# 48 of the 128 pieces of wo's last row on three partitions, loaded ahead of the rest of wo by three DMA engines

## The chip, the cores and the metric

The kernel runs on one core of one Trainium2 chip. The metric is the device time of one execution in microseconds; lower is better. The kernel before takes 382.13 us (median of three runs, 381.94 to 382.17). Its profiled execution took 382.16 us, and the profile's span of it is 380.7 us long.

The engines are called PE (TensorE, matrix products), DVE (VectorE), ACT (ScalarE), POOL (GpSimd) and SP (SyncE, which here only issues DMA transfers). SBUF is the memory on the chip in which all tiles lie, with 128 partitions; PSUM receives the results of PE. One core has sixteen DMA engines, which share the work of every large transfer.

## The reference, cut to what matters

One token `x` of 1024 features goes through two branches, which a gate mixes. Branch A is attention of 32 query heads over a cache of 65,536 keys and values in four groups of heads; branch B is a gated MLP for one position. All inputs are bf16.

```python
def reference(A_x, A_k_cache, A_v_cache, A_wq, A_wo, B_x, B_w_in, B_w_sp, B_b_sp, B_w_out, gate_w):
    # A_k_cache, A_v_cache: [1, 4, 65536, 128]; A_wq: [1024, 4096]; A_wo: [4096, 1024]
    def _A_ref(x, k_cache, v_cache, wq, wo):
        q = (x @ wq) as 32 heads of 128                     # (shortened)
        k, v = k_cache, v_cache repeated 8 times over heads  # (shortened)
        scores = jnp.einsum('bhqd,bhkd->bhqk', q, k) * Dh ** (-0.5)
        p = _softmax(scores, axis=-1)
        o = jnp.einsum('bhqk,bhkd->bhqd', p, v)
        return o.reshape(B, Sq, Hq * Dh) @ wo                # (transposes left out)
    ...
    g = _sigmoid((x * gate_w).sum(-1, keepdims=True))
    a = _A_ref(x, A_k_cache, A_v_cache, A_wq, A_wo)
    b = _B_ref(x, B_w_in, B_w_sp, B_b_sp, B_w_out)
    return g * a + (1 - g) * b
```

The last step of branch A, a vector of 4096 times `wo`, is what the change touches.

## The kernel before

All large inputs pass through one SBUF tile, `kv`, of five slots of 16,384 bf16 elements per partition. SP issues every load in program order into it; a load waits until the slot's former contents have been read. The order is: w_in, wq, the first K tiles, w_out, then K and V by groups, the last group's V in three loads, and last `wo` in five.

```python
P = 128
CT = 128
NKV = 5
...
WO_SPLIT = (24, 4, 2, 1, 1)
WO_BUSY = {24: 0, 4: 2, 2: 1, 1: 0}
...
    kv = big.tile([P, NKV * CT * P], BF16, name="kv")

    def load(src, shape, at):
        ...
        v = kv[:, int(at * CT * P):int(at * CT * P) + n]
        ...
        ins = nc.sync.dma_start(out=v, in_=src)
        ...
        return v
```

`wo` is seen as 128 partitions of 32 rows (partition p holds rows 32p to 32p+31 of `wo`), so a "row of wo" below is one row index c of all 128 partitions: 128 pieces of 1024 bf16 elements, 2 KB each, 256 KB in all. `project` multiplies one such row after the other with the attention output `oa` [128, 32], in four column blocks which go to four 32-row strips of PSUM, and adds it all up in `out_ps`. `keep_busy` issues matmuls on old data whose result nobody reads.

```python
    def keep_busy(n):
        ps = pss.tile([P, 2 * HN], FP32, name="busy_ps", tag="s")
        w = wt[G % 2][:].rearrange("p v b t u h -> p (v b t u h)")
        for i in range(n):
            ins = nc.tensor.matmul(ps[:, :HN], lhsT=w[:, :P], rhs=w[:, :HN], start=True,
                                   stop=True, skip_group_check=True)
            if i > 0:
                same_weights(ins)          # the repeated weight load is dropped

    NO = D // NB                           # 256
    out_ps = psl.tile([P, NO], FP32, name="out_ps")

    def project(w, n, vec, c0, first=False, last=False):
        for c in range(n):
            for t in range(NB):            # NB = 4
                nc.tensor.matmul(
                    out_ps[t * B:(t + 1) * B, :],
                    lhsT=vec[:, c0 + c:c0 + c + 1].to_broadcast([P, B]),
                    rhs=w[:, c, t * NO:(t + 1) * NO],
                    start=(first and c == 0), stop=(last and c == n - 1),
                    skip_group_check=True)
```

The end of the kernel: the last group's V in slots 2 and 3, then slot 1, then slot 0; the attention output; `wo` in rows of 24, 4, 2, 1 and 1 from slot 3 on; and the store.

```python
    for j, n, at in ((0, 2, 2), (2, 1, 1), (3, 1, 0)):
        for i, vt in enumerate(load_kv(A_v_cache, G - 1, j, at, n)):
            v_tile(G - 1, j + i, vt)
    keep_busy(6)
    head_out(G - 1)
    keep_busy(16)


    wo_view = A_wo.rearrange("(p c) n -> p c n", c=OC)      # OC = 32
    c0 = 0
    for n in WO_SPLIT:
        t = load(wo_view[:, c0:c0 + n, :], (n, D), 3 + c0 * D / (CT * P))
        project(t, n, oa, c0, last=(c0 + n == OC))
        keep_busy(WO_BUSY[n])
        c0 += n
    out_sb = const.tile([P, NO], BF16, name="out_sb")
    ...
    nc.scalar.copy(out=out_sb[:], in_=out_ps[:])
    for i, queue in enumerate((nc.scalar, nc.sync)):
        ...                                # two stores of 1 KB
```

`head_out(g)` (not shown) normalises the attention output of one group on DVE and PE, and writes `oa`. At the start the token and `gate_w` are loaded by ACT's queue as 8 partitions of 256 bytes each, and two single numbers (`B_w_sp`, `B_b_sp`) as one element each.

Of the kernel before, what the change touches and what calls it, by code (L numbers as in the profile page):

```python
# [8 lines left out]
FP32 = mybir.dt.float32  # L9
BF16 = mybir.dt.bfloat16  # L10
I32 = mybir.dt.int32
ACT = mybir.ActivationFunctionType
ALU = mybir.AluOpType
AX = mybir.AxisListType
# [4 lines that stand above are left out]
B = 32  # L19
NB = P // B  # L20
VC = 4
CC = CT // VC
ZN = 448
HN = 512
WO_SPLIT = (24, 4, 2, 1, 1)
WO_BUSY = {24: 0, 4: 2, 2: 1, 1: 0}


# [1 line left out]
def kernel(  # L30
# [15 lines left out]
    nc = tc.nc  # L46

    _, _, D = A_x.shape
    _, G, S, DH = A_k_cache.shape
# [7 lines left out]
    OC = HD // P  # L57
# [3 lines left out]
    NHB = HD // (NB * HN)  # L61
# [1 line left out]
    SCALE = float(DH) ** -0.5  # L63
    assert NB * VC * REP == P and G * B == P and B == REP * QD and DH == P and D % P == 0
    assert S % (P * CT) == 0 and F == 2 * NB * ZN and ZN == B * FC and HD == NHB * NB * HN
    assert NHB * NB == 2 * G and CC * B == 2 * HN and sum(WO_SPLIT) == OC

    const = ctx.enter_context(tc.tile_pool(name="const", bufs=1))
    wk = ctx.enter_context(tc.tile_pool(name="wk", bufs=2))
# [4 lines left out]
    psm = ctx.enter_context(tc.tile_pool(name="psm", bufs=1, space=bass.MemoryType.PSUM))  # L74
# [5 lines left out]
    def same_weights(ins):  # L80
        held.add(ins.ins.name)
# [93 lines left out]
    kv = big.tile([P, NKV * CT * P], BF16, name="kv")  # L175

    def load(src, shape, at):
        n = 1
        for s in shape:
            n *= s  # L180
        v = kv[:, int(at * CT * P):int(at * CT * P) + n]
        if len(shape) == 2:
            v = v.rearrange("p (a b) -> p a b", b=shape[1])
        ins = nc.sync.dma_start(out=v, in_=src)  # L184
        if not first_load:
            first_load.append(ins.ins.name)
        return v

    def load_kv(src, g, j, at, n=1):
        h, i = divmod(j, 2)  # L190
        rows = src[0, g, 2 * h * CT * P:2 * (h + 1) * CT * P, :].rearrange(
            "(p c) d -> p (c d)", c=2 * CT)
        v = load(rows[:, i * CT * DH:(i + n) * CT * DH], (n * CT * DH,), at)
        return [v[:, i * CT * DH:(i + 1) * CT * DH] for i in range(n)]
# [18 lines left out]
    row = const.tile([P, P], FP32, name="row")  # L213
    nc.gpsimd.iota(row[:], pattern=[[1, P]], base=0, channel_multiplier=0,
                   allow_small_or_imprecise_dtypes=True)
    pidx = const.tile([P, 1], I32, name="pidx")
# [7 lines left out]
    for t in wt:  # L224
        nc.gpsimd.memset(t[:], 0.0)

    pbits = const.tile([P, 6], I32, name="pbits")
    for i, m in enumerate((P // KC - 1, B - 1, QD - 1, REP - 1)):
        nc.vector.tensor_scalar(out=pbits[:, i:i + 1], in0=pidx[:], scalar1=m, scalar2=None,
                                op0=ALU.bitwise_and)  # L230
    nc.vector.tensor_scalar(out=pbits[:, 4:5], in0=pidx[:], scalar1=B.bit_length() - 1,
                            scalar2=None, op0=ALU.logical_shift_right)
    nc.vector.tensor_scalar(out=pbits[:, 5:6], in0=pidx[:], scalar1=REP.bit_length() - 1,
                            scalar2=2 * VC - 1, op0=ALU.logical_shift_right, op1=ALU.bitwise_and)
    pf = const.tile([P, 7], FP32, name="pf")
    nc.vector.tensor_copy(out=pf[:, 0:1], in_=pidx[:])
    nc.vector.tensor_copy(out=pf[:, 1:7], in_=pbits[:])

    def one_hot(shape, dtype, in0, col, name):
        t = const.tile(shape, dtype, name=name)  # L240
        nc.vector.tensor_scalar(out=t[:], in0=in0, scalar1=pf[:shape[0], col:col + 1],
                                scalar2=None, op0=ALU.is_equal)
        return t
# [9 lines left out]
                     start=True, stop=True)  # L253
    xm = const.tile([P, 2, KC, P // KC], FP32, name="xm")
    for t in range(2):
        nc.vector.tensor_tensor(  # L256
            out=xm[:, t], in0=xb_ps[:, t * P:(t + 1) * P].rearrange("p (i c) -> p c i", c=KC),
            in1=sel_i[:].unsqueeze(1).to_broadcast([P, KC, P // KC]), op=ALU.mult)
# [17 lines left out]
                            op0=ALU.add)  # L276
    nc.vector.reciprocal(out=gw[:, 2:3], in_=gw[:, 1:2])
    nc.vector.tensor_scalar(out=gw[:, 5:6], in0=gw[:, 2:3], scalar1=-1.0, scalar2=1.0,
                            op0=ALU.mult, op1=ALU.add)
# [4 lines left out]
    nc.vector.tensor_copy(out=own_bb[:], in_=own_b[:].unsqueeze(1).to_broadcast([P, NB, B]))  # L284
    own_8 = one_hot([P, 2 * VC], FP32, row[:, :2 * VC], 6, "own_8")
    own_q = one_hot([P, QD], FP32, row[:, :QD], 3, "own_q")
    hsel = one_hot([P, REP, QD], FP32, row[:, :REP].unsqueeze(2).to_broadcast([P, REP, QD]), 4,
                   "hsel")

# [20 lines left out]
    for hf in range(2):  # L310
        nc.vector.tensor_tensor(
            out=zm[:, hf], in0=z_ps[:, hf * HN:hf * HN + ZN].rearrange("p (j c) -> p j c", c=FC),
            in1=own_b[:].unsqueeze(2).to_broadcast([P, B, FC]), op=ALU.mult)
    z = wk.tile([P, 2 * FC], FP32, name="z")
    nc.vector.tensor_reduce(out=z[:].rearrange("p (h c) -> p h c", h=2),
                            in_=zm.rearrange("p h j c -> p h c j"), axis=AX.X, op=ALU.add)
# [3 lines left out]
                            op0=ALU.mult, op1=ALU.add)  # L320
# [4 lines left out]
                            op0=ALU.mult, op1=ALU.add)  # L325
# [12 lines left out]
                            scalar2=None, op0=ALU.mult)  # L338
    nc.vector.tensor_tensor(out=stat[:, 2:3], in0=stat[:, 0:1], in1=stat[:, 0:1], op=ALU.mult)
    nc.vector.tensor_tensor(out=stat[:, 3:4], in0=stat[:, 1:2], in1=stat[:, 2:3],  # L340
                            op=ALU.subtract)
    nc.vector.tensor_scalar(out=stat[:, 4:5], in0=stat[:, 3:4], scalar1=1e-5, scalar2=None,
                            op0=ALU.add)
# [4 lines left out]
                            op0=ALU.subtract, op1=ALU.mult)  # L348
    nc.vector.tensor_scalar(out=z2n[:], in0=z2n[:], scalar1=wsp, scalar2=bsp,
                            op0=ALU.mult, op1=ALU.add)  # L350
    uT = const.tile([P, FC], BF16, name="uT")
    nc.vector.scalar_tensor_tensor(out=uT[:], in0=zg[:, 0:FC], scalar=gate1, in1=z2n[:],
                                   op0=ALU.mult, op1=ALU.mult)
# [40 lines left out]
    oa = const.tile([P, OC], BF16, name="oa")  # L394
# [54 lines left out]
    def v_tile(g, j, vt):  # L449
        if j == 0:  # L450
            o_ps[g] = pso.tile([P, 2, VC * DH], FP32, name="o_ps")
        vx = vt.rearrange("p (v c d) -> p c v d", v=VC, d=DH)
        for u in range(CC // 2):
            hs = slice(u % 2 * P // 2, (u % 2 + 1) * P // 2)
            for e in range(2):
                ins = nc.tensor.matmul(  # L456
                    o_ps[g][hs, e, :],
                    lhsT=ptt[g, j][:, 2 * u:2 * u + 2, :].rearrange("p c x -> p (c x)"),
                    rhs=vx[:, 2 * u + e], start=(j == 0 and u < 2),
                    stop=(j == NT - 1 and u >= CC // 2 - 2), skip_group_check=True)  # L460
                if e > 0:
                    same_weights(ins)
# [35 lines left out]
                same_weights(ins)  # L498
# [4 lines left out]
    def project(w, n, vec, c0, first=False, last=False):  # L503
        for c in range(n):
            for t in range(NB):
                nc.tensor.matmul(  # L506
                    out_ps[t * B:(t + 1) * B, :],
                    lhsT=vec[:, c0 + c:c0 + c + 1].to_broadcast([P, B]),
                    rhs=w[:, c, t * NO:(t + 1) * NO],
                    start=(first and c == 0), stop=(last and c == n - 1),  # L510
                    skip_group_check=True)
# [3 lines left out]
    for j, n, at in ((0, 1, 2), (1, 1, 3), (2, 1, 0), (3, 1, 1)):  # L515
        for i, kn in enumerate(load_kv(A_k_cache, 0, j, at, n)):
            k_tile(0, j + i, kn)
        if j == 1:
            build_w(1)
    project(load(B_w_out.rearrange("(p c) n -> p c n", c=FC), (FC, D), 4), FC, uT, 0, first=True)  # L520
    stats(0)
    for g in range(1, G):
# [12 lines left out]
    for j, n, at in ((0, 2, 2), (2, 1, 1), (3, 1, 0)):  # L535
        for i, vt in enumerate(load_kv(A_v_cache, G - 1, j, at, n)):
            v_tile(G - 1, j + i, vt)
    keep_busy(6)
    head_out(G - 1)
    keep_busy(16)  # L540


    wo_view = A_wo.rearrange("(p c) n -> p c n", c=OC)
    c0 = 0
    for n in WO_SPLIT:
        t = load(wo_view[:, c0:c0 + n, :], (n, D), 3 + c0 * D / (CT * P))
        project(t, n, oa, c0, last=(c0 + n == OC))
        keep_busy(WO_BUSY[n])
        c0 += n
    out_sb = const.tile([P, NO], BF16, name="out_sb")  # L550
    out_rows = out.rearrange("o t (q n) -> (o t q) n", n=NO)
    nc.scalar.copy(out=out_sb[:], in_=out_ps[:])  # L552
# [5 lines left out]
    last = {}  # L558
# [37 lines left out]
```

## Time and profile before

| What | Value |
| --- | --- |
| time | 382.13 us (381.94 to 382.17) |
| span of the profile | 380.7 us, 2605 instructions |
| PE busy | 233.2 us (61%), 1395 matmuls |
| DVE busy | 218.5 us (57%) |
| ACT busy | 39.6 us (10%) |
| packets of the DMA engines | 3943, of 162.17 MB |
| chain that ended last, by engine | DMA 57%, PE 26%, DVE 13%, ACT 2% |

How to read it: busy time is an average over the whole span, so a share of 61% doesn't say that PE has slack at each point. The chain follows the last instruction back to what released it, step by step, and tells whose work set the end. A transfer is listed at its issue, and its length runs to its landing; much of that is time in the queue behind other transfers.

In the timeline a row has: start in us, length in us, engine, line, operation, tile written and tiles read, shape, count, and in brackets the idle time before it and what ended it.

### The profile page before, as it was taken

Reading aid. Unit: us, or ns where it says so; the run is one execution under the profiler, and the core shown is the slowest. Engines: PE = TensorE matmul, PEld = TensorE weight load, DVE = VectorE, ACT = ScalarE, POOL = GpSimd, SP = SyncE. Lnnn points to the kernel's source line nnn. Section 1 sums busy time; section 2 is a strip of 40 time slices with the busy share of each in tenths; the row PEclk is TensorE's granted clock in tenths of the full one; section 3 lists DMA queues with packets and bytes.
Section 4 is the critical chain, followed back from the end, with each engine's and each line's share of the span. In section 5 each row is a group of like instructions: output and inputs, shape, how many; then the busy total and the mean of one; then the engine's idle time right before and its main releaser. Section 6 shows DMA issues by size and latency. Waiting matters only on the chain.

```text
span 380.7 us, 2605 instructions
## 1 busy us (share of the span) xinstructions
PE 233.2 (61%) x1395; PEld 56.0 (15%) x800; DVE 218.5 (57%) x211; ACT 39.6 (10%) x55; POOL 4.4 (1%) x10
## 2 busy tenths in 40 slices
PE   0060657876157944796397729871977196839386
PEld 0010101111101210111011101120211011202113
DVE  4133288997597506966977059669970388460040
ACT  1001001110601100114010001050100000500000
POOL 4000000000000000000000000000000000000000
PEclk9995769899759895989688958895989579969789
DMA  9998999999999999999999999999999999999995
GB/s 386 496 420 379 411 438 441 437 483 430 387 420 441 441 436 441 427 441 441 434 436 441 441 427 434 406 423 441 434 434 429 420 441 442 436 410 430 424 443 223
DMA packets 3943, 162.17 MB, mean 426 GB/s; under 512 B 472, under 2 KB 476, under 8 KB 860
## 3 DMA queue, kind: packets, MB, share of 16 engines
q1 hardware_dynamic: 3892, 162.01, 98.8%
q8 instruction: 8, 0.13, 0.1%
q14 instruction: 3, 0.02, 0.0%
q10 hardware_dynamic: 40, 0.01, 0.0%
HBM read 162.01 MB, written 0.00 MB: 426 GB/s over the span
## 4 chain that ended last, share of the span: by engine, by line
DMA 57%; PE 26%; DVE 13%; ACT 2%; issue 1%; SPq 1%; DVEq 0%; ACTq 0%
DMA kv<-in_A_k_cache_dram 43%; PE s_ps L410 21%; DMA kv<-in_A_wo_dram 7%; DVE kv L403 7%; DMA kv<-in_A_v_cache_dram 7%; PE o_ps L456 4%; DVE pt L446 2%; DVE o_sb L470 1%; DVE mx L405 1%; ACT sc L421 1%; ACT sc L443 1%; DVE rowt L466 1%; SPq L184 1%; PE om_ps L476 0%; DVE osum L486 0%
## 5 line engine op out<-in xcount | busy, mean ns | idle before, releaser
L410 PE MATMUL s_ps<-kv,wt 128*128 128x512 bf16 x512 | 141.8, 437 | 80.2 <-DVE kv L403 80.2
L403 DVE STREAM_TRANSPOSE kv<-kv 128x2048 int32<-128x2048 int32 x64 | 142.7, 2281 | 54.3 <-DMA kv<-in_A_k_cache_dram 54.3
L456 PE MATMUL o_ps<-kv,pt 128*64 128x512 bf16 x512 | 61.7, 400 | 7.6 <-DMA kv<-in_A_v_cache_dram 7.6
L410 PEld LDWEIGHTS <-wt 128*128 128x128 bf16 x256 | 27.6, 108 | 195.6 <-issue 138.5
L421 ACT CAST sc<-s_ps 128x1024 bf16<-128x1024 f32 x16 | 16.2, 1012 | 249.9 <-PE s_ps L410 249.9
L456 PEld LDWEIGHTS <-pt 128*64 128x64 bf16 x256 | 16.1, 115 | 50.6 <-issue 48.1
L446 DVE STREAM_TRANSPOSE pt<-sc 128x1024 bf16<-128x1024 bf16 x16 | 18.6, 1217 | 6.8 <-ACT sc L443 6.8
L405 DVE TENSOR_REDUCE mx<-sc 128x1 f32<-128x1024 bf16 x12 | 14.5, 1210 | 9.9 <-ACT sc L421 9.9
L443 ACT ACTIVATE sc<-sc,nb 128x1024 bf16<-128x1024 bf16 x16 | 18.2, 1137 | 12.3 <-DVE nb L439 12.2
L466 DVE TENSOR_TENSOR rowt<-o_ps,own 128x1024 f32<-128x1024 f32 x4 | 4.8, 1195 | 24.9 <-PE o_ps L456 24.9
L476 PE MATMUL om_ps<-o_sb,hsel 128*32 128x128 f32 x8 | 2.3, 386 | 18.3 <-DVE o_sb L470 18.3
L425 DVE TENSOR_REDUCE mx<-sc 128x1 f32<-128x1024 bf16 x4 | 4.9, 1220 | 13.6 <-ACT sc L421 13.6
L296 PE MATMUL q_ps<-kv,xT 128*32 128x512 bf16 x64 | 5.6, 527 | 7.2 <-DMA kv<-in_A_wq_dram 7.2
L252 PE MATMUL xb_ps<-xg,spread 8*128 8x256 bf16 x1 | 0.4, 366 | 13.2 <-DMA xg<-in_gate_w_dram 13.2
L470 DVE TENSOR_REDUCE o_sb<-rowt 128x128 f32<-128x1024 f32 x4 | 7.5, 1872 | 0.1
L363 DVE TENSOR_TENSOR rowt<-q_ps,own_b 128x512 f32<-128x512 f32 x2 | 1.3, 686 | 10.8 <-PE q_ps L296 10.8
L296 PE MATMUL z_ps<-kv,xT 128*32 128x448 bf16 x64 | 5.9, 560 | 0.0
L495 PE MATMUL busy_ps<-wt 128*128 128x512 bf16 x23 | 5.8, 381 | 0.1
L506 PE MATMUL out_ps<-kv,oa 128*32 128x256 bf16 x128 | 4.2, 274 | 2.0 <-DMA kv<-in_A_wo_dram 2.0
L256 DVE TENSOR_TENSOR xm<-xb_ps,sel_i 128x128 f32<-128x128 f32 x2 | 0.5, 287 | 8.0 <-PE xb_ps L252 8.0
L552 ACT CAST out_sb<-out_ps 128x256 bf16<-128x256 f32 x1 | 0.4, 372 | 45.1 <-PE out_ps L506 45.1
L296 PEld LDWEIGHTS <-xT 128*32 128x32 bf16 x64 | 2.6, 136 | 14.6 <-issue 14.6
(90 smaller groups left out, 59.3 us busy)
## 6 DMA issues: line engine op xcount, KB each, us to landing
kv<-in_A_k_cache_dram SPq DMA_DIRECT2D x4, 4096.0 KB, 35.4
kv<-in_A_v_cache_dram SPq DMA_DIRECT2D x2, 4096.0 KB, 26.0
kv<-in_B_w_in_dram SPq DMA_DIRECT2D x1, 7168.0 KB, 19.4
kv<-in_A_wo_dram SPq DMA_DIRECT2D x1, 6144.0 KB
kv<-in_B_w_out_dram SPq DMA_DIRECT2D x1, 3584.0 KB
kv<-in_A_wo_dram SPq DMA_DIRECT2D x1, 1024.0 KB
kv<-in_A_wo_dram SPq DMA_DIRECT2D x1, 512.0 KB
kv<-in_A_wo_dram SPq DMA_DIRECT2D x2, 256.0 KB, 28.2
```

The source lines that it names most:

```text
L296: ins = nc.tensor.matmul(ps[t * B:(t + 1) * B, k * HN:k * HN + n], lhsT=xT[:, i * KH + c:i * KH + c + 1].to_broadcast([P, B]), rhs=w[:, c, ...
L403: nc.vector.transpose(out=kb[:, v * n:(v + 1) * n], in_=kb[:, v * n:(v + 1) * n])
L405: nc.vector.reduce_max(**late.pop())
L410: ins = nc.tensor.matmul(s_ps[:, k * HN:(k + 1) * HN], lhsT=wt[g % 2][:, v, b].rearrange("p a v h -> p (a v h)"), rhs=kx[:, b // 2, b % 2, ...
L421: nc.scalar.copy(out=sct[g, j][:], in_=s_ps[:])
L425: nc.vector.reduce_max(**late.pop())
L443: nc.scalar.activation(out=sct[g, j][:], in_=sct[g, j][:], func=ACT.Exp, scale=SCALE, bias=nb[:, 0:1], accum_out=lss[g][:, j:j + 1])
L446: nc.vector.transpose(out=ptt[g, j][:].rearrange("p c x -> p (c x)"), in_=sct[g, j][:])
L456: ins = nc.tensor.matmul(o_ps[g][hs, e, :], lhsT=ptt[g, j][:, 2 * u:2 * u + 2, :].rearrange("p c x -> p (c x)"), rhs=vx[:, 2 * u + e], sta ...
L466: nc.vector.tensor_tensor(out=om8, in0=o_ps[g][:].rearrange("p e (v d) -> p (e v) d", d=DH), in1=own_8[:].unsqueeze(2).to_broadcast([P, 2 ...
L470: nc.vector.tensor_reduce(out=o_sb[:], in_=om8.rearrange("p x d -> p d x"), axis=AX.X, op=ALU.add)
L495: ins = nc.tensor.matmul(ps[:, :HN], lhsT=w[:, :P], rhs=w[:, :HN], start=True, stop=True, skip_group_check=True)
```

## The change

`wo`'s last row (c = 31) is no longer one transfer of 128 pieces. 48 of its pieces, those of the partitions whose number leaves 3, 5 or 7 on division by 8, go to three other partitions, 0, 8 and 16, sixteen pieces to each, in slot 2, which the first V tile of the last group has left. This transfer is issued ahead of the other rows of `wo`. The other 80 pieces stay on their own partitions and come last, in two transfers (partitions 1, 9, 17, ... and all even ones). The idea is to shorten what the sixteen DMA engines have to move at the very end, by giving three of them a share of it earlier.

To multiply the moved pieces, the matching 48 numbers of `oa`'s last column must be brought to partitions 0, 8 and 16, sixteen in each: a small matmul with a constant 0/1 matrix (`to_port`) does that, from a masked spread of the column over sixteen columns (`oa_e`). The other 80 keep their place, and the column used for them (`oa_last[:, 1:2]`) is zero where a piece was moved. The moved rows are multiplied first, in 16 x 4 matmuls with 24 rows each, of which 21 hold zeros in the vector. The number of filler matmuls after the attention output goes from 16 to 6 and 2.

```diff
-WO_SPLIT = (24, 4, 2, 1, 1)
+WO_SPLIT = (24, 4, 2, 1)
+PORT, PORTS, ENGINES = 8, 3, 16
...
-    pbits = const.tile([P, 6], I32, name="pbits")
+    pbits = const.tile([P, 8], I32, name="pbits")
...         (two more bit fields, three more columns of pf)
+    to_port = one_hot([P, PORT * PORTS], BF16, row[:, :PORT * PORTS], 9, "to_port")
+    own_e = one_hot([P, ENGINES], BF16, row[:, :ENGINES], 7, "own_e")
...
+    wo_view = A_wo.rearrange("(p c) n -> p c n", c=OC)
+    last_row = wo_view[:, OC - 1, :]
+    NM = PORT * PORTS
+    moved = kv[:NM, 2 * CT * P:2 * CT * P + ENGINES * D].rearrange("p (e d) -> p e d", d=D)
+    nc.sync.dma_start(out=moved[::PORT],
+                      in_=last_row.rearrange("(e r) d -> r e d", r=PORT)[3::2])
     keep_busy(6)
     head_out(G - 1)
-    keep_busy(16)
-
-
-    wo_view = A_wo.rearrange("(p c) n -> p c n", c=OC)
+    oa_last = wk.tile([P, 2], BF16, name="oa_last")
+    nc.vector.tensor_tensor(out=oa_last[:], in0=pf[:, 10:12],
+                            in1=oa[:, OC - 1:OC].to_broadcast([P, 2]), op=ALU.mult)
+    oa_e = wk.tile([P, ENGINES], BF16, name="oa_e")
+    nc.vector.tensor_tensor(out=oa_e[:], in0=own_e[:],
+                            in1=oa_last[:, 0:1].to_broadcast([P, ENGINES]), op=ALU.mult)
+    keep_busy(6)
+    mv_ps = psm.tile([NM, ENGINES], FP32, name="mv_ps", tag="m")
+    nc.tensor.matmul(mv_ps[:], lhsT=to_port[:], rhs=oa_e[:], start=True, stop=True)
+    oa_moved = wk.tile([NM, ENGINES], BF16, name="oa_moved")
+    nc.vector.tensor_copy(out=oa_moved[:], in_=mv_ps[:])
+    keep_busy(2)
+    project(moved, ENGINES, oa_moved, 0)
+
     c0 = 0
     for n in WO_SPLIT:
         t = load(wo_view[:, c0:c0 + n, :], (n, D), 3 + c0 * D / (CT * P))
-        project(t, n, oa, c0, last=(c0 + n == OC))
+        project(t, n, oa, c0)
         keep_busy(WO_BUSY[n])
         c0 += n
+    t = kv[:, (3 * CT * P + c0 * D):(3 * CT * P + (c0 + 1) * D)]
+    for r, step in ((1, PORT), (0, 2)):
+        nc.sync.dma_start(out=t[r::step], in_=last_row[r::step])
+    project(t.unsqueeze(1), 1, oa_last[:, 1:2], 0, last=True)
```

More of the change, by code (lines that the diff above doesn't have):

```diff
@@ L65 @@
     assert S % (P * CT) == 0 and F == 2 * NB * ZN and ZN == B * FC and HD == NHB * NB * HN
-    assert NHB * NB == 2 * G and CC * B == 2 * HN and sum(WO_SPLIT) == OC
+    assert NHB * NB == 2 * G and CC * B == 2 * HN and sum(WO_SPLIT) == OC - 1 and PORT * ENGINES == P
     const = ctx.enter_context(tc.tile_pool(name="const", bufs=1))
@@ L234 @@
                             scalar2=2 * VC - 1, op0=ALU.logical_shift_right, op1=ALU.bitwise_and)
-    pf = const.tile([P, 7], FP32, name="pf")
+    nc.vector.tensor_scalar(out=pbits[:, 6:7], in0=pidx[:], scalar1=PORT.bit_length() - 1,
+                            scalar2=None, op0=ALU.logical_shift_right)
+    nc.vector.tensor_scalar(out=pbits[:, 7:8], in0=pidx[:], scalar1=1, scalar2=None,
+                            op0=ALU.bitwise_and)
+    pf = const.tile([P, 12], FP32, name="pf")
     nc.vector.tensor_copy(out=pf[:, 0:1], in_=pidx[:])
-    nc.vector.tensor_copy(out=pf[:, 1:7], in_=pbits[:])
+    nc.vector.tensor_copy(out=pf[:, 1:9], in_=pbits[:])
     def one_hot(shape, dtype, in0, col, name):
@@ L286 @@
     own_q = one_hot([P, QD], FP32, row[:, :QD], 3, "own_q")
+    nc.vector.tensor_scalar(out=pf[:, 9:10], in0=pf[:, 4:5], scalar1=float(PORT // 2),
+                            scalar2=-1.5 * PORT, op0=ALU.mult, op1=ALU.add)
+    nc.vector.tensor_scalar(out=pf[:, 10:11], in0=pf[:, 4:5], scalar1=3.0, scalar2=pf[:, 8:9],
+                            op0=ALU.is_ge, op1=ALU.mult)
+    nc.vector.tensor_scalar(out=pf[:, 11:12], in0=pf[:, 10:11], scalar1=-1.0, scalar2=1.0,
+                            op0=ALU.mult, op1=ALU.add)
+    to_port = one_hot([P, PORT * PORTS], BF16, row[:, :PORT * PORTS], 9, "to_port")
+    own_e = one_hot([P, ENGINES], BF16, row[:, :ENGINES], 7, "own_e")
     hsel = one_hot([P, REP, QD], FP32, row[:, :REP].unsqueeze(2).to_broadcast([P, REP, QD]), 4,
@@ L507, in project @@
                     out_ps[t * B:(t + 1) * B, :],
-                    lhsT=vec[:, c0 + c:c0 + c + 1].to_broadcast([P, B]),
+                    lhsT=vec[:, c0 + c:c0 + c + 1].to_broadcast([vec.shape[0], B]),
                     rhs=w[:, c, t * NO:(t + 1) * NO],
```

## The prediction

> **What bounds the kernel now.** I read four views, in this order: the page's slices, its chain and its queues; then the timeline of the last eight microseconds; then the trace's DMA packet records one by one.
>
> The slices first. In these two rows each digit is the busy share of one fortieth of the span, in tenths.
>
> ```profile
> DMA  9998999999999999999999999999999999999995
> GB/s 386 496 420 379 411 438 441 437 483 430 387 420 441 441 436 441 427 441 441 434 436 441 441 427 434 406 423 441 434 434 429 420 441 442 436 410 430 424 443 223
> HBM read 162.01 MB, written 0.00 MB: 426 GB/s over the span
> ```
>
> The DMA engines are full from start to end: the kernel is a stream of 162 MB, and only the last slice shows a tail. The tail is in the timeline (start, length, engine, operation, idle before):
>
> ```profile
> 373.50 3.24 PE L506 MATMUL out_ps<-kv,oa 128*32 128x256 bf16 x112 [1.39 <-DMA kv<-in_A_wo_dram]
> ...
> 378.58 0.29 PE L506 MATMUL out_ps<-kv,oa 128*32 128x256 bf16 x4 [0.35 <-DMA kv<-in_A_wo_dram]
> ...
> 378.92 0.37 ACT L552 CAST out_sb<-out_ps 128x256 bf16<-128x256 f32 x1 [45.10 <-PE out_ps L506]
> ```
>
> The last four matmuls wait for wo's last row to land. After that come only 0.3 us of matmul, 0.37 us of copy and the store. So a last landing that comes x us later makes the kernel x us longer, and one that comes earlier makes it shorter by as much. The chain of waits agrees on what ends last:
>
> ```profile
> 350.26 28.28 DMA kv<-in_A_wo_dram
> 378.54 0.04 issue
> 378.58 0.32 PE out_ps L506 x4
> ```
>
> [...] The semaphore records give the sixteen landings of the last row:
>
> ```
> first eight : 376.46 376.61 376.62 376.63 376.71 376.75 376.95 377.14
> last eight  : 378.00 378.03 378.08 378.13 378.17 378.37 378.38 378.54
> ```
>
> Two groups, 1.5 us apart. This is the slack the change is after: eight engines sit idle while eight still carry wo. Who is late, and why? The page lists two small queues beside the kernel's own:
>
> ```profile
> q1 hardware_dynamic: 3892, 162.01, 98.8%
> q8 instruction: 8, 0.13, 0.1%
> q14 instruction: 3, 0.02, 0.0%
> ```
>
> The packets carry no engine number, but on one engine each packet starts 3 to 4 ns before its predecessor ends, so I chained them into sixteen lanes. Each of the eight 16 KB instruction packets (at 43, 97, 136, 194, 248, 291, 332 and 376 us) falls into a different lane. It takes about 1.05 us and the next packet there about 0.5 us more than its usual 2.42 us: that lane stays about 1.5 us late to the end. Seven fetches make seven late lanes; the eighth lane got two 8 KB fetches. The eighth 16 KB fetch starts at 376.15 us, just as its lane has sent its last wo data, and costs nothing.
>
> To number the lanes I used the small loads at the start: the two 8-partition loads (x, gate_w) put one 256-byte packet into each of eight lanes, and the single-element loads all go to one of these. Some lanes run within 2 ns of each other and can be swapped, but group by group the count fits: the lanes hit by the 16 KB fetches are those same eight, and the single-element lane is hit last, at 376.15.
>
> [...] 8 packets of 16,384 bytes, about 280 PE instructions apart on average. [...] No view of this kernel shows ports; a 49,152-byte packet takes 1.819 us, 27.0 GB/s[...].
>
> **The change part by part.**
>
> 1. Less on all sixteen engines. Wo's last row shrinks from 8 pieces per engine to 5 (one from the 16-partition DMA, four from the 64-partition one). A 2 KB packet takes 84 ns, and the last row's eight take 377.41 to 378.08 us in the latest lane, 0.083 each: 3 x 0.083 = 0.25 us saved.
>
> 2. More on engines 0, 1, 2. Sixteen pieces each, queued behind V and ahead of wo: 16 x 0.083 = 1.33 us. Net there: +1.08 us.
>
> 3. Where these three stand. If the numbering holds, engine 0 is an early lane (last data sent at 376.15 us), while engines 1 and 2 are late ones. The late lanes that got a 16 KB fetch sent their last data at 377.52, 377.57, 377.64, 377.68, 377.71, 377.88 and 377.94 us. The first and last fetched of them are the 377.88 and the 377.94, and engine 1, next to engine 0 in a running order, should be one of these: 377.9 + 1.08 = 379.0 us. The end before was 378.08, so the last data comes 0.9 us later.
>
> 4. The fetch that was harmless. 16 x 4 matmuls with as many weight loads are 128 PE instructions ahead of the 24-row part; 16 filler matmuls with one load become 8 with two. Net about +123. [...]it arrived at 376.15, with PE about 180 instructions into its work on wo. It will now be asked for about 123 instructions sooner, during the work on the moved pieces (about 371 us), and reach engine 0 near 373. Then engine 0 ends at 376.15 + 1.08 + 1.5 = 378.7: no longer early.
>
> 5. Ports. Engine 2 writes the moved pieces to partition 16, [...]which is busy with wo's 24-row part. If the two halve it, the 1.33 us become up to 2.6 for engine 2[...]. Engine 2: 377.6 + 1.08 + 1.3 = 380.0, 1.9 us later than before. [...]
>
> 6. Compute. Attention output is ready at 369.89. Two small DVE products and one small copy at about 0.16 us, one matmul at about 0.3: PE can start on the moved pieces near 371. 64 matmuls at 3.24 / 112 = 0.029 us are 1.9 us, done near 373, before the 24-row part lands (373.46 before, later now). That costs nothing. If the 24 rows land at 375 to 375.5, their 96 matmuls (2.8 us) still end ahead of the last landing at 379 to 380. Three more DMA issues on SP (0.42 us each) fall some 30 us before their landing. The extra DVE constants come in the start, when DVE idles 8 us for the first load.
>
> Sum: -0.25 for the late engines that aren't loaded; for the three that are, +0.9 without port sharing, +1.9 with it.
>
> **The rivals.**
>
> First rival: engines 0 to 2 are early lanes. For it: somebody chose exactly three engines and 48 pieces; 3 pieces off each and 13 net on three fit a lag of 1.5 us (18 pieces). Then the early lanes reach 376.2 + 1.08 = 377.3, the late ones set the end at -0.25 us, and the time is 381.9. Against it: the small loads mark the same eight lanes as the fetches. I give it one in eight.
>
> Second rival: [...]the 5-piece rest suffers too[...]. That eats up to 0.4 us on the others and changes nothing for engine 2: 384.0. I give sharing that costs most of a microsecond a little under a half.
>
> Third rival: the landing of the 24 rows, held up on three engines, pushes PE past the last landing. The sums of part 6 leave a microsecond or more: unlikely, and it would add to the others.
>
> **Range and chances.** No sharing: 382.13 + 0.9 = 383.0. Full sharing: 384.0. First rival: 381.9. Weighted at about 0.45, 0.42 and 0.13 that is 383.3; the 80% range, 382.0 to 384.3, takes in nearly all three. Two per cent are 7.6 us, more than any of these, so "within 2%" is all but certain.
>
> **What would show it.** The last row's landings: if I am right, the two latest belong to engines 1 and 2 and come at 379.4 or later, a group of two or three standing apart behind the rest, and the others end about 0.25 us sooner than now. Port sharing would show as 2 KB packets of about 168 ns instead of 84 behind V's last piece near 358 to 361 us, and as longer 48 KB packets in one other lane. The eighth 16 KB fetch near 373 us would confirm part 4. The 64 new matmuls should stand at 371 to 373 us. I am wrong if all landings come within 0.5 us of each other and the end is earlier; then the numbering of the lanes failed. I am also wrong if the chain's last wait is for PE or DVE and not for a landing of wo.

## The result, and the profile after

| | before | after |
| --- | --- | --- |
| median time | 382.07 us (6 runs) | 383.70 us (6 runs, 383.54 to 384.42) |
| span of the profile | 380.7 us | 382.2 us |
| last row of wo landed | 378.54 us | 378.82 us |
| PE ended | 378.90 us | 380.44 us |

The ratio is 1.0047 (1.0034 to 1.0060): the changed kernel is slower by about 1.6 us. The predicted 383.3 us is 0.4 us off. Yet in the profiles the last row landed only 0.28 us later, and PE ended 1.54 us later. So most of the loss does not come from where the prediction looked for it.

The page's slices after the change (granted clock of PE, busy share of the DMA engines):

```profile
PEclk9995769899759895989588959895989589969698
DMA  9998999999999999999999999999999999999994
```

The DMA engines are as full as before. New is the PEclk row at its end. The same row of the kernel before:

```profile
PEclk9995769899759895989688958895989579969789
```

Its last slice, in which wo is multiplied, was 9 and is now 8. (The slices of 7 and 8 ahead of it, now 6 and 9, share one stretch of half clock, 357 to 364 us, which both kernels have.) The chain of waits after the change (start, length, engine, tile and line):

```profile
348.56 25.38 DMA kv<-in_A_wo_dram
373.94 0.04 issue
373.98 4.91 PE out_ps L519 x112
378.89 0.54 PE busy_ps L508 x2
379.43 0.33 PE out_ps L519 x8
379.76 0.32 PE busy_ps L508
380.08 0.36 PE out_ps L519 x8
```

Before, the chain's last transfer was wo's last row, landing at 378.54. Now it is the transfer of 24 rows, landed at 373.94, and from there on PE never waits for a landing: 112 matmuls (28 rows of wo), two fillers, two rows, one filler, the last two rows. PE has become the bound. The timeline of the same stretch (start, length, engine, operation, idle before):

```profile
371.10 1.93 PE L519 MATMUL out_ps<-kv,oa_moved 24*32 24x256 bf16 x64
373.98 4.91 PE L519 MATMUL out_ps<-kv,oa 128*32 128x256 bf16 x112 [0.95 <-DMA kv<-in_A_wo_dram]
380.13 0.28 PE L519 MATMUL out_ps<-kv,oa_last 128*32 128x256 bf16 x4
```

The block of 112 matmuls is the same work as before, which took 3.24 us from 373.50. It now takes 4.91 us. The sum is closed by three terms: 0.48 us from the later landing of the 24 rows (373.98 against 373.50), 1.67 us from the slower block (4.91 against 3.24), less 0.61 us of slack that PE had before. That slack: without the last wait PE would have ended at 373.50 + 3.24 + 1.55 (the tail in the chain above: 0.54 + 0.33 + 0.32 + 0.36) = 378.29 instead of 378.90. 0.48 + 1.67 - 0.61 = 1.54 us, the measured delay of PE's end.

Why is the block slower? The records of the granted clock step at intervals of 3.413 us, so I laid windows on these steps (window, length, then busy us and count of PE, PEld, DVE, ACT and POOL, then the clock granted to PE, the DMA share and GB/s). Before:

```profile
367.11:370.52 3.41, 2.37 (x12) 0.23 (x3) 2.18 (x6) 0.00 (x0) 0.00 (x0) 1.00 0.97 418
370.52:373.94 3.42, 2.03 (x25) 0.53 (x21) 0.00 (x0) 0.00 (x0) 0.00 (x0) 1.00 0.91 380
373.94:377.35 3.41, 3.19 (x109) 2.76 (x103) 0.00 (x0) 0.00 (x0) 0.00 (x0) 1.00 0.86 333
```

After:

```profile
367.25:370.67 3.42, 2.02 (x10) 0.42 (x5) 2.48 (x8) 0.00 (x0) 0.00 (x0) 1.00 0.90 388
370.67:374.08 3.41, 2.46 (x70) 1.72 (x72) 0.16 (x1) 0.00 (x0) 0.00 (x0) 1.00 0.90 380
374.08:377.49 3.41, 3.41 (x68) 3.16 (x70) 0.00 (x0) 0.00 (x0) 0.00 (x0) 0.50 0.88 342
377.49:380.50 3.01, 2.92 (x71) 1.53 (x58) 0.00 (x0) 0.04 (x1) 0.00 (x0) 1.00 0.06 20
```

For exactly one stretch, 374.08 to 377.49, PE was granted half its clock (0.50), and this stretch lies inside the block of 112. Half of 3.413 us is 1.71, which covers the 1.67. The matmuls in it start at distances of about 33, 7, 6 and 168 ns in each group of four, against 16, 3, 4 and 86 ns in the full-clock stretch behind it: all about doubled, so it is the clock and not a stall here and there.

The odd thing is in the second row of each table: in the stretch ahead of the half clock PE was *busier* after (2.46 us) than before (2.03 us). PE was busy for 72% of that stretch, and half a clock followed it. That is what the experiments had to clear up.

The transfers. The semaphore records give the landings of the largest part of the last row (even partitions) after the change, sorted:

```
376.24 376.42 376.47 377.38 377.76 377.85 377.88 377.90
377.91 377.93 378.09 378.10 378.26 378.34 378.36 378.82
```

The moved pieces are 2 KB packets behind V's last packet in three lanes. Their first packets start at 356.53, 356.68 and 357.17 us, whereas in the late lanes wo's first packets start at 357.93 to 358.55. So the three engines are *early* lanes. Two lanes carry their packets in 84 to 94 ns each, and the third like this (ns, sixteen packets from 356.53 us on):

```
seven packets of 84 to 87, then 171 178 178 179 178 168 171 180 179
```

That lane's next 48 KB packet took 2.156 us, and in an unmoved lane one 48 KB packet that started at 356.30 took 2.791 us and the next 2.022 us, against 1.816 to 1.840 us everywhere else. The two lanes were slow at the same time: the nine slow packets ran from 357.1 to 358.6 us, the packet of 2.791 us from 356.30 to 359.09. The slowed lane took 2.06 us for its sixteen packets instead of 1.32, and 0.33 us more for the next: it lost 1.07 us. The other lost 0.97 + 0.20 = 1.17 us. The slowed lane is the one that lands at 378.82, and its part of the 24 rows is the 373.94 that PE waits for; the other fifteen parts had landed by 373.53.

### The profile page after: what moved, and what is told of

Same layout as the page of the kernel before. It is cut to its first block, busy times and chain, and to the rows that moved or that the text cites. A ratio compares the mean times of both kernels' runs of the same rounds, so it can differ in the third digit from the quotient of the medians.

```text
span 382.2 us, 2742 instructions
## 1 busy us (share of the span) xinstructions
PE 235.2 (62%) x1454; PEld 58.8 (15%) x866; DVE 219.6 (57%) x221; ACT 39.6 (10%) x55; POOL 4.4 (1%) x10
## 4 chain that ended last, share of the span: by engine, by line
DMA 56%; PE 27%; DVE 13%; ACT 2%; issue 1%; SPq 0%; DVEq 0%; ACTq 0%
DMA kv<-in_A_k_cache_dram 42%; PE s_ps L423 21%; DVE kv L416 7%; DMA kv<-in_A_v_cache_dram 7%; DMA kv<-in_A_wo_dram 7%; PE o_ps L469 4%; DVE pt L459 2%; PE out_ps L519 1%; DVE o_sb L483 1%; DVE mx L418 1%; ACT sc L434 1%; ACT sc L456 1%; DVE rowt L479 1%; PE om_ps L489 0%; PE busy_ps L508 0%
## 5 line engine op out<-in xcount | busy, mean ns | idle before, releaser
L519 PE MATMUL out_ps<-kv,oa 128*32 128x256 bf16 x124 | 5.6, 350 | 1.0 <-DMA kv<-in_A_wo_dram 1.0
L519 PEld LDWEIGHTS <-oa 128*32 128x32 bf16 x124 | 4.7, 124 | 2.1 <-issue 1.8
```

Of the source, the lines that this page charges most:

```text
L519: nc.tensor.matmul(out_ps[t * B:(t + 1) * B, :], lhsT=vec[:, c0 + c:c0 + c + 1].to_broadcast([vec.shape[0], B]), rhs=w[:, c, t * NO:(t + 1 ...
```

## The experiments

I began with two theories, called D and P in the expectations: D, the loss comes from the transfers; P, it comes from the new matmuls on the moved pieces. The first four kernels were to tell these apart. After them I formed theory A, on the clock: what sets it goes by how much of PE's array is filled, not by whether PE is busy, and the change took out the fillers (128 x 128 weights, 512 columns) and put in matmuls that fill next to nothing (24 x 32 weights, 256 columns). In the expectations f1, f2 and f4 are the kernels of experiments 5, 6 and 8. There, "own ports" is the author's name for partitions 0, 4 and 8 (or 0 to 11) in place of 0, 8 and 16, and "port sharing" that for the slowing of two lanes at the same time; no trace shows a port.

### 1. The transfers alone

```diff
     keep_busy(2)
-    project(moved, ENGINES, oa_moved, 0)
```

The products of the 48 moved pieces are left out of the output.

> The changed kernel without the 64 matmuls on the moved pieces (their 48 products are left out of the sum); all transfers as in the change. Theory P (the 64 matmuls bring PE's granted clock to one half from 374.1 to 377.5 us, so that the 24 rows take 4.9 us instead of 3.2 and PE ends last): the clock stays full, the last matmuls wait for the last landing near 378.8 us, time 382.1 to 382.6. Theory D (later landings of wo set the end): nothing changes, 383.5 to 384.

Measured: 383.91 us (383.52 to 384.50, 4 runs), ratio 1.0049 (1.0034 to 1.0064), as slow as the whole change although 64 matmuls are gone. The windows:

```profile
369.09:372.50 3.41, 0.92 (x4) 0.28 (x3) 0.64 (x4) 0.00 (x0) 0.00 (x0) 1.00 0.85 365
372.50:375.91 3.41, 2.09 (x41) 1.75 (x44) 0.00 (x0) 0.00 (x0) 0.00 (x0) 0.50 0.96 387
375.91:379.32 3.41, 3.41 (x72) 2.86 (x64) 0.00 (x0) 0.00 (x0) 0.00 (x0) 0.50 0.37 142
```

Now two stretches have half the clock, and the chain's last block is longer still:

```profile
373.82 5.91 PE out_ps L519 x109
```

The last landing came at 378.68, 0.14 us after the one before. So the 64 matmuls don't cost the time (P falls in its plain form). The time is the one that D expected, but D's cause isn't there either: PE ends at 381.27, 2.6 us after the last landing. With less work on PE, the clock fell sooner: at 372.50 us, and at 374.08 after the change.

### 2. The compute alone

The last row is again one transfer and nothing is moved; the matmuls on the moved pieces run on old data with a vector of zeros.

```diff
-    nc.vector.tensor_scalar(out=pf[:, 10:11], in0=pf[:, 4:5], scalar1=3.0, scalar2=pf[:, 8:9],
+    nc.vector.tensor_scalar(out=pf[:, 10:11], in0=pf[:, 4:5], scalar1=300.0, scalar2=pf[:, 8:9],
-    nc.sync.dma_start(out=moved[::PORT],
-                      in_=last_row.rearrange("(e r) d -> r e d", r=PORT)[3::2])
...
-    for r, step in ((1, PORT), (0, 2)):
-        nc.sync.dma_start(out=t[r::step], in_=last_row[r::step])
+    nc.sync.dma_start(out=t, in_=last_row)
```

> The changed kernel's compute with the transfers of the kernel before: nothing is moved, wo's last row comes as one transfer, the 64 matmuls run on old data with a vector of zeros. Theory P: half clock after 374 us again and PE ends last, 383.4 to 384. Theory D: 382.0 to 382.3 as before the change.

Measured: 383.16 us (382.86 to 384.43, 5 runs), ratio 1.0034 (1.0020 to 1.0047). The windows:

```profile
370.81:374.22 3.41, 2.91 (x90) 2.23 (x92) 0.12 (x1) 0.00 (x0) 0.00 (x0) 1.00 0.85 356
374.22:377.64 3.42, 3.42 (x75) 3.09 (x68) 0.00 (x0) 0.00 (x0) 0.00 (x0) 0.50 0.81 309
```

PE's block starts at 373.62 and takes 4.91 us as after the change, at half the clock, with the transfers as before. So some 1.0 of the 1.6 us are there without any moved piece. Of the missing 0.6, 0.36 us lie (in the profiles) in the landing of the 24 rows: it comes at 373.58 here and not at 373.94.

### 3. Partitions 0, 4 and 8

They stand in place of 0, 8 and 16, to see whether the slow packets go with the choice of partitions.

```diff
+STEP = 4
-                            scalar2=-1.5 * PORT, op0=ALU.mult, op1=ALU.add)
+                            scalar2=-1.5 * STEP, op0=ALU.mult, op1=ALU.add)
...         (STEP for PORT in to_port, NM and the factor, too)
-    nc.sync.dma_start(out=moved[::PORT],
+    nc.sync.dma_start(out=moved[::STEP],
```

> The moved pieces go to partitions 0, 4 and 8 instead of 0, 8 and 16[...]. If ports were shared in the change, no 48 KB packet takes 2.8 us any more, 2 KB packets all take about 84 ns, and the last landing comes 0.3 to 0.5 us sooner. Theory P: the time stays at 383.5 to 384 because PE ends last anyway. Theory D: 383.0 to 383.4.

Measured: 382.30 us (381.76 to 383.93 over 20 runs), ratio 1.0007 (1.0000 to 1.0013). That is below what either theory expected. Not one 2 KB packet took over 120 ns, and the longest 48 KB packet behind the moved pieces took 1.815 us: the slow packets are gone. They are gone in experiment 12 as well, where `kv` begins at the same byte as after the change, so they came from the choice of partitions. But the time can't be credited to that. The whole stream ran faster, from the first K tile on: the usual 64 KB packet took 2.418 us against 2.421 (some 2.428) in the kernels so far. `to_port` is narrower here, by 24 bytes per partition, and with padding `kv`, which is allocated behind it, begins at byte 28,416 of a partition instead of 28,448. Experiments 9, 10 and 12 follow this up. The clock had halved here too in the profiled execution, for two stretches; that it does so in some executions only would fit the spread of 2.2 us over the runs (mean granted clock 0.826 in the slowest, 0.852 in the fastest).

### 4. No filler ahead of the moved pieces

```diff
-    keep_busy(6)
...
-    keep_busy(2)
```

> The change without the 8 filler matmuls between the attention output and the moved pieces. Theory P in the form that all PE work of the microseconds before counts: 2 us less of it, the clock stays full after 374 us, 382.2 to 382.7. In the form that only the matmuls on moved pieces bring the clock down: 383.5 to 384. Theory D: 383.5 to 384.

Measured: 384.41 us (384.34 to 384.55, 4 runs), ratio 1.0062 (1.0047 to 1.0077): the slowest of all, and above what any theory expected. The timeline:

```profile
371.29 3.51 PE L519 MATMUL out_ps<-kv,oa_moved 24*32 24x256 bf16 x64 [0.25 <-DVE oa_moved L568]
...
374.73 4.94 PE L519 MATMUL out_ps<-kv,oa 128*32 128x256 bf16 x112
```

Half the clock from 371.43 to 378.25, two stretches: the 64 small matmuls take 3.51 us instead of 1.93. With less filler the clock fell sooner, at 371.43 us and not at 374.08; theory A took shape here.

### 5. The fillers back

```diff
-    keep_busy(6)
+    keep_busy(8)
     mv_ps = psm.tile([NM, ENGINES], FP32, name="mv_ps", tag="m")
...
     project(moved, ENGINES, oa_moved, 0)
+    keep_busy(6)
```

With the `keep_busy(2)` that stands ahead of `project(moved, ...)` these are sixteen, as before the change.

> The change with 16 filler matmuls again (8, 2, and 6 after the moved pieces) instead of 8. Theory A (PE's clock falls to one half after a window of 3.4 us with little array work; the 64 matmuls on 24 rows of 128 count for little, and it is the 8 missing fillers that let it fall): full clock from 364 us on, the last matmuls wait for the last landing near 378.8 us, 382.2 to 382.6. Theory P (the 64 matmuls themselves bring it down): half clock, 383.5 to 384.5.

Measured: 382.73 us (382.32 to 383.69, 20 runs), ratio 1.0014 (1.0007 to 1.0021): 1.0 us better than the change by the medians, from eight more matmuls whose results nobody reads. The windows:

```profile
370.69:374.11 3.42, 3.37 (x71) 1.68 (x66) 0.16 (x1) 0.00 (x0) 0.00 (x0) 1.00 0.89 375
374.11:377.52 3.41, 3.10 (x98) 2.54 (x100) 0.00 (x0) 0.00 (x0) 0.00 (x0) 1.00 0.89 345
```

The clock stays full. The chain shows what is left:

```profile
373.49 1.03 PE busy_ps L508 x4
374.51 2.19 PE out_ps L519 x76
376.70 0.32 issue
377.01 1.17 PE out_ps L519 x36
```

The fillers run on until 374.5, past the landing of the 24 rows at 373.92, and there is a stall of 0.3 us in the block that no recorded wait explains. It stands behind the 76th matmul here and in experiments 6 and 12, and PE goes on 1.45, 1.37 and 1.43 us after a 16 KB instruction packet has ended (375.56, 373.70 and 375.53 us); so PE probably waited for its instructions, which isn't tested. PE still ends last, at 379.73, and not on a landing as theory A expected; the time is 0.1 us above its range.

### 6. The fillers back, and partitions 0, 4 and 8

Experiments 3 and 5 together.

> As f1, and the moved pieces go to partitions 0, 4 and 8[...]. Theory A with port sharing undone: the last landing comes from a late lane with three pieces less, near 378.2 us, 381.7 to 382.0. If the own ports bring nothing: as f1.

Measured: 381.77 us (381.01 to 382.73, 12 runs), ratio 0.9986 (0.9977 to 0.9995): faster than before. Last landing 377.46, PE's end 377.82. At first sight this rescues the idea of the change; but `kv` begins at byte 28,416 here again, and the stream is the fast one.

### 7. The kernel before, with eight fillers fewer

Nothing of the change but the number of fillers.

```diff
-    keep_busy(16)
+    keep_busy(8)
```

> The kernel before with 8 filler matmuls after the attention output instead of 16; nothing else of the change. Theory A: the window from about 370.5 us holds little array work, half clock after 374, 383.2 to 384.2. Theory P: 382.0 to 382.3 as before.

Measured: 383.28 us (382.46 to 384.57, 14 runs), ratio 1.0029 (1.0021 to 1.0038). The windows:

```profile
367.42:370.83 3.41, 2.24 (x10) 0.33 (x4) 2.09 (x6) 0.00 (x0) 0.00 (x0) 1.00 0.90 389
370.83:374.25 3.42, 0.60 (x24) 0.60 (x27) 0.00 (x0) 0.00 (x0) 0.00 (x0) 1.00 0.88 368
374.25:377.66 3.41, 3.41 (x75) 3.06 (x68) 0.00 (x0) 0.00 (x0) 0.00 (x0) 0.50 0.81 312
```

And the chain:

```profile
373.65 4.91 PE out_ps L506 x112
```

The same 4.91 us as after the change. That eight missing fillers halve the clock for one stretch, and that this alone makes the kernel 1.0 us slower, is shown by this pair of kernels, which differ in one number.

That the share of the array decides it is a fit, not a single comparison. For each stretch I added up weight rows / 128 x weight columns / 128 x data columns / 512: a filler (0.216 us) is 1, so that 16 fill a stretch; a matmul on wo is 1/8, one on the moved pieces 1/43 (1/85 where it takes 12 rows). The stretch just ahead of the decision that counts for the block on wo, in all kernels (numbered as the experiments), ordered by this share of the array:

```
kernel            stretch from  share of array  share of time  next clock
4 (no filler)        368.01        0.02                          half
1 (transfers)        369.09        0.13             0.27         half
7 (before, 8 fill.)  370.83        0.19             0.18         half
after                370.67        0.19             0.72         half
3 (0, 4 and 8)       367.46        0.23             0.87         half
2 (compute)          370.81        0.34             0.85         half
6                    367.99        0.36                          full
12                   370.52        0.36                          full
5 (fillers back)     370.69        0.41             0.99         full
9                    368.85        0.50                          full
before               370.52        0.51             0.59         full
10                   369.75        0.51                          full
11                   370.24        0.70                          full
8                    370.48        0.82                          full
```

Busy time does not order them (0.59 stays full, 0.87 falls); the share of the array does, with a border near 0.35. One earlier stretch breaks it: 0.32 in kernel 3, from 364.04, kept the full clock. The same sum over all 1446 stretches between 3 and 376 us of the fourteen traces (a matmul that crosses a step is counted in part) says more: all 448 stretches below 0.31 were followed by half the clock, all 929 above 0.39 by the full clock, whichever clock they had themselves, and the 69 in between went both ways; a border at 0.38 has 12 stretches on the wrong side. So the share of the array is a good account of the clock in these traces; busy time fails mainly where small matmuls fill the time. The steps lie at another phase in every execution, so a kernel near the border can fall on one side or the other. That may be the spread of kernel 3, but not that of kernel 6, whose slowest run had the higher mean clock (0.848, and 0.838 in the profiled one, among the fastest).

### 8. Sixteen matmuls instead of sixty-four

Twelve partitions (0 to 11), four pieces on each, in four transfers of three partitions: the matmuls take 12 rows at a time, and there are 16 of them. 18 fillers.

```diff
+STEP, EACH = 4, 4
...
+    picked = last_row.rearrange("(e r) d -> r e d", r=PORT)[3::2]
+    for i in range(STEP):
+        nc.sync.dma_start(out=moved[i::STEP], in_=picked[:, i * EACH:(i + 1) * EACH])
...
-    keep_busy(6)
+    keep_busy(8)
...
-    project(moved, ENGINES, oa_moved, 0)
+    project(moved, EACH, oa_moved, 0)
+    keep_busy(8)
```

> As f2, with the moved pieces four to each of partitions 0 to 11 (four transfers of three partitions[...]), so 16 matmuls for them instead of 64, and 18 fillers. Theory A: as f2, 381.7 to 382.0; the number of matmuls for the moved pieces does not matter as long as the clock is kept.

Measured: 381.11 us (380.93 to 382.39, 8 runs), ratio 0.9976 (0.9965 to 0.9987), faster than expected. Full clock; the fillers end at 372.86, the last landing is at 377.13, PE ends at 377.59. Again `kv` begins at 28,416, and the packets are those of 2.418 us.

### 9. The kernel before, with `kv` 32 bytes further on

Nothing of the change; one constant tile is made wider, so that `kv` begins at byte 28,160 instead of 28,128. The new columns are not used.

```diff
-    pf = const.tile([P, 7], FP32, name="pf")
+    pf = const.tile([P, 15], FP32, name="pf")
```

> The kernel before with one constant tile (pf) widened by 32 bytes per partition, so that the kv tile starts at byte 28160 of each partition, a multiple of 64, instead of 28128. Nothing else. Theory K (the start of kv decides the pace of every load: the three kernels so far whose 64 KB packets took 2.418 us are the three with kv at a multiple of 64, byte 28416; all with kv at 28128 or 28448 show 2.421 to 2.428 us): packets of 2.418 us, the stream 0.7 to 1.1 us shorter, 381.0 to 381.5. If the faster pace came with the own ports: 382.0 to 382.4.

Measured: 380.99 us (380.85 to 381.06, 6 runs), ratio 0.9968 (0.9957 to 0.9980): 1.2 us faster than the kernel before, and the fastest of all. The page and then the chain:

```profile
HBM read 162.01 MB, written 0.00 MB: 427 GB/s over the span
```

```profile
349.04 28.49 DMA kv<-in_A_wo_dram
377.52 0.04 issue
377.57 0.32 PE out_ps L506 x4
```

The last landing is at 377.52 instead of 378.54. 1694 of the 1792 64 KB packets take 2.418 us, and the mean is 2.4204 against 2.4247 us. A lane carries 1792 / 16 = 112 of them: 112 x 0.0043 = 0.5 us. The 48 KB packets (1.815 us against 1.816 to 1.826) and the instruction packets (0.93 against 1.07 us) are shorter as well. All packets added up, one engine carries 0.93 us less on average, and the last landing came 1.02 us sooner. The bytes 28,160 and 28,416 are multiples of 64, 128 and 256, while 28,128 and 28,448 are multiples of 32 only; which of these boundaries counts, the runs can't tell.

### 10. Experiment 8 with `kv` off the boundary

`pf` 32 bytes wider, so that `kv` is back at 28,448, the start it has in the changed kernel; six fillers at the end instead of eight.

```diff
-    pf = const.tile([P, 12], FP32, name="pf")
+    pf = const.tile([P, 20], FP32, name="pf")
...
-    keep_busy(8)
+    keep_busy(6)
```

> As f4 (16 matmuls, own ports) with 16 fillers, 6 of them after the moved pieces, and pf widened so that kv starts at byte 28448, off a multiple of 64 as in the kernel before. Theory K: packets of 2.421 to 2.428 us again; the moved pieces alone are then worth the three pieces taken from the late lanes, about 0.25 us: 381.7 to 382.1. If the pace came with the own ports: 380.8 to 381.2.

Measured: 382.02 us (381.82 to 382.11, 13 runs), ratio 0.9994 (0.9986 to 1.0002). This is the idea of the change with all three side effects taken away (the clock, partitions 0, 8 and 16, the start of `kv`). Its chain:

```profile
359.96 18.35 DMA kv<-in_A_wo_dram
378.31 0.04 issue
378.36 0.32 PE out_ps L521 x4
```

The last landing is 0.23 us earlier than before, where part 1 of the prediction has 0.25. One profile says little here: with the transfers unchanged the last landing is at 378.54 (before), 378.66 (experiment 2) and 378.69 (experiment 7); with the moved pieces on partitions 0 to 11 it is at 378.31 here, and with them on 0, 4 and 8 at 378.38 in experiment 12, 0.28 us earlier on average. In time the gain is 0.2 us by the medians, and the interval reaches from a gain of 0.5 us to a loss of 0.1. So the idea itself is worth about 0.2 us in this form, if anything.

### 11. Experiment 8 with six fillers at the end

`kv` stays at 28,416.

> As f4 with 6 fillers after the moved pieces instead of 8, kv at byte 28416. The 8 fillers ended at 372.8 us, 0.4 us after the 24 rows had landed; with 6 the 24 rows start on landing: 380.7 to 381.1.

Measured: 381.06 us (380.75 to 381.41, 7 runs; an eighth took 482.53 us and is left out), ratio 0.9971 (0.9961 to 0.9982). The last landing is at 377.27, 0.25 us earlier than in experiment 9. The time is no better than that of experiment 9, which has nothing of the change: on the good start of `kv` the moved pieces bring no gain in time that these runs can show. Against experiment 10 only the start of `kv` differs: 1.0 us faster by the medians.

### 12. Experiment 6 with `kv` off the boundary

```diff
-    pf = const.tile([P, 12], FP32, name="pf")
+    pf = const.tile([P, 20], FP32, name="pf")
```

> As f2 (64 matmuls, own ports, 16 fillers) with kv at byte 28448 instead of 28416. Against f1 it differs in the ports alone. Theory K: 382.3 to 382.7, so that most of the 1.0 us between f1 and f2 was the start of kv, and the ports are worth 0.1 to 0.4 us. If the ports made the difference: 381.6 to 381.9.

Measured: 382.48 us (381.86 to 383.39, 13 runs), ratio 1.0009 (1.0001 to 1.0017). Against experiment 6 only the start of `kv` differs: 0.7 us slower by the medians. Against experiment 5 only the partitions of the moved pieces differ (`to_port` is narrower and `pf` wider here, but `kv` begins at the same byte): the last landing is at 378.38 instead of 378.81, so in these two profiles partitions 0, 8 and 16 cost 0.43 us of landing. In time it can't be told: both kernels end with PE, at 379.68 and 379.73. The chain of experiment 12:

```profile
374.37 2.19 PE out_ps L520 x76
376.56 0.41 issue
```

The fillers again overshoot the landing, and the same stall stands in the block.

## Why the prediction was right or wrong

The time was nearly right by luck: most of the loss came from a term that the working had set to zero, and the landing that it had put 0.9 to 1.9 us later came 0.28 us later. Point by point:

**Part 1, 0.25 us less on all engines: right in size.** Experiments 10 and 12 show 0.28 us on average at the last landing.

**Part 2, 16 x 0.083 us on three engines: right.** The two undisturbed lanes carry their sixteen packets in 1.32 and 1.31 us.

**Part 3, "If the numbering holds": failed.** The three engines are early lanes, in the changed kernel (first moved packets at 356.53 to 357.17 us) and in every experiment that moves pieces. Which engines carry three partitions was the author's assumption, as was the order of the lanes; the packets carry no engine number. The working itself said that some lanes run within 2 ns of each other and can be swapped; one in eight for the first rival, which had it right, took that too lightly. Which engines the instruction packets fall on stays open.

**Part 4, the harmless fetch: half right.** The eighth 16 KB packet moved from 376.15 to 374.32 us (predicted about 373), and a ninth follows at 377.79. That the fetches go by a count of instructions was the author's estimate: between two of the 16 KB fetches the traces of before and after have 142 to 432 recorded PE instructions. Which engine it met isn't settled, so its cost in this kernel isn't either.

**Part 5, ports: nearly right in size, on one lane; the cause was not shown.** Packets of 168 to 180 ns were measured where 168 were named, though only for the last nine of the sixteen, and then in the lane's next 48 KB packet too: 1.1 us and 1.2 us were lost in the two lanes, where up to 1.3 was predicted for one. Why the two slowed together no trace shows, only that the slow packets went with partitions 0, 8 and 16 (experiments 3 and 12). As the lanes were early ones, most of it was swallowed by their lead: the end came 0.28 us later, not 1.9. The second rival's addition, that the remaining pieces suffer from sharing as well, isn't seen: of the remaining 2 KB packets 196 took 80 to 89 ns, 11 took 90 to 99, one 105.

**Part 6, compute: "That costs nothing" is the step that failed.** The working looked only at when PE is free: 64 matmuls, 1.9 us, done near 373. That was right, to 371.10 and 1.93 us. But the same change took 8 of 16 fillers away, and the fillers kept the clock up (experiments 5 and 7). Their place was filled in time and not in the array, so the clock fell to half for 3.41 us, and the block counted at "2.8 us" for its 96 matmuls, 3.24 for 112, took 4.91. That is +1.67 us, and experiment 7 gets it with no other part of the change. The third rival, PE pushed past the last landing and called unlikely, is what happened: by its own cause (0.48 us of a later landing) it would have used up only the slack of 0.61 us, and with the clock it went over.

So the transfers, which were to make all of +1.2 us, made +0.28 at the last landing of these two profiles. Four profiles with the change's transfers (after, experiments 1, 4 and 5) against the three with the old ones put it at 0.13 us on average. The term that was set to zero made most of the rest. The sentence "I am also wrong if the chain's last wait is for PE or DVE and not for a landing of wo" describes the outcome. The page of before had a hint: a helper called `keep_busy`, whose results nobody reads, called with 16, and a PEclk row that dips to 5 and 7 elsewhere in the span.

## What to carry to other kernels

Matmuls whose result nobody reads kept the clock up here: with eight fewer of them it fell to half for 3.41 us, and the kernel took 1.0 us longer (experiment 7). Before replacing them by real work, count how much of the array that work fills in each 3.41 us, not how long PE is busy. When few DMA engines send to few partitions, try other partitions and look at the packets: on 0, 8 and 16 nine of the 2 KB packets took 168 to 180 ns, on 0, 4 and 8 none took over 120 (experiment 3). And look at the byte at which a large DMA target begins: here 32 bytes in a constant's width were worth 1.2 us, more than the whole idea of the change, and any edit that resizes an earlier tile can move it unseen.

## What the runs showed of the hardware that I had not expected

- The clock of PE halved after stretches of 3.41 us in which PE was busy for 72 to 87% of the time, where its matmuls filled little of the array (0.19 to 0.34 by the sum of experiment 7 in these three kernels). In all fourteen traces a share under 0.31 was always followed by half the clock, and one over 0.39 never.
- The start of the target tile within a partition changed the rate of the whole stream: 2.418 us for the usual 64 KB packet at bytes 28,160 and 28,416, 2.421 to 2.428 at 28,128 and 28,448, and 1.2 us of the kernel's time (experiment 9). It is the written side that differs there, while the source is the same.
- Two lanes slowed at the same time when three lanes wrote to partitions 0, 8 and 16: in one, nine 2 KB packets took 168 to 180 ns instead of 84, in the other a 48 KB packet took 2.79 us instead of 1.82.
